# Q, k and v of token blocks two to four as pairs of 64-row matmuls with two PSUM sums each

## The chip, the core and the metric

One core of a Trainium2 chip runs the whole program. Its engines work side by side: TensorE (PE; its weight loads are listed as PEld), VectorE (DVE), ScalarE (ACT), GpSimd (POOL) and SyncE (SP), which issues the DMAs here. TensorE writes its sums to PSUM, which has eight banks of 128 x 512 fp32; VectorE and ScalarE read them. The metric is the device time of one execution in microseconds; the lower the better.

## The reference

```python
x = A_x                                  # 1 x 2048 x 576
xn = layernorm(x)
qkv = xn @ wqkv                          # 576 x 1728, 32 heads of 18
p = softmax(q @ k.T * 18 ** -0.5)
s = (p @ v) @ wo
g = silu((gelu(xn @ w_gate) * (xn @ w_up)) @ w_down)   # 4608 hidden
out = x + s * g
```

Everything is fp32. The kernel works in a reduced-mantissa format (fp32r) on parts: an operand is split into a high part and the low part that is left, and a product is the sum of high by high, low by high and high by low.

## The kernel before

The tokens are cut into NB = 4 blocks of TB = 512, written b = 0 to 3 in the code and first to fourth here. A first stage (the pools `pro` and `pps`) makes the layernorm, transposes xn and computes q, k and v; it stores q and k in DRAM (`qk`) as high and low parts, v in DRAM (`vs`), and the transposed xn (`xhs`). A second stage, some 2240 us long, runs the gate and up products interleaved with attention, and a third the output projection. This change is in the first stage, which ends at about 196 us.

For one block the first stage does this:

- `load_x` fetches four row tiles of x, `norm` (line 203) makes their statistics (`bn_stats`, `bn_aggr`), the reciprocal root, and scales them; the last 64 columns are copied behind each tile, so that the rest of the rows is 128 wide.
- `transposes` (line 234) makes 20 PE transposes into five PSUM tiles `pt`; `split_t` (line 185) splits each into a high part by ScalarE (`xt[0]`) and a low part by VectorE (`xt[1]`). The 576 rows are KT = 4 full tiles and 64 left over; the fifth tile, `xt[2]`, holds the high part of those 64 rows in partitions 0 to 63 and the low part in 64 to 127.
- `project` (line 286) computes one 128-row tile of q or k for the 512 tokens of a block; nine of these per block, in the order `ORDER`. `mm_terms` (line 174) issues 14 matmuls of 128 rows: for each of the four full row tiles high by high, low by high, high by low, and two for the fifth tile, whose 128 rows hold high and low at once. ScalarE takes the sum's high part (`t1`), VectorE the low part (`t2`); both have three buffers (`tmp2`, line 182) and are stored to `qk`.
- `values_of` (line 295) computes v of 128 tokens and half the heads, 288 columns; eight per block, 14 matmuls each. ScalarE copies the sum to one of eight buffers `VN`, which is stored to `vs`.
- `store_xt` (line 246) stores the transposed x of the block; for the first block `load_xd` (line 136) loads it back as `xd`, in 64-row pieces, for the gate and up products; `load_gu` (line 122) fetches the first tile of gate and up weights, `split_gu` splits it.

The loop at line 347 goes through the blocks: nine `project`; `norm` of the next block after the fifth of these; `store_xt`; the next block's `transposes`; eight `values_of`. PE's order is that of the program (`manual_schedule`, line 74). On the other engines a scheduler places the instructions, except those that are wrapped in `keep_in_program_order`: they stay in the order in which the program issues them, among themselves. So before, VectorE may do the norm of a later block as soon as its x has landed. A tile pool with `bufs` = n gives a new tile the buffer of an old one, and the first instruction that writes it waits until the old one has been read.

In the second stage `gate_up` (line 403) already runs pairs: two matmuls of 64 rows, one on the upper and one on the lower half of PE's rows, one after the other in program order and with a sum of their own (`pg`, `pu`). So do the attention scores (`pm`, `pe`, lines 698 and 729) and the down products (`py`, line 465).

Of the kernel before, what the change touches and what calls it, by code (L numbers as in the profile page):

```python
# [8 lines left out]
F32 = mybir.dt.float32  # L9
F32R = mybir.dt.float32r  # L10
AF = mybir.ActivationFunctionType
ALU = mybir.AluOpType
# [42 lines left out]
def f(ap):  # L55
    return ap.bitcast(F32)
# [13 lines left out]
def kernel(ctx: ExitStack, tc: tile.TileContext, x, wqkv, wo, w_gate, w_up, w_down, out):  # L70
# [65 lines left out]
    def load_xd(b, key=None):  # L136
# [11 lines left out]
        return xd  # L148


    TERMS = [(0, k, 0) for k in range(KT)] + [(1, k, 0) for k in range(KT)] + [(0, k, 1) for k in range(KT)] \
        + [(0, KT, 2), (1, KT, 2)]

    FIRST_TERMS = sorted(TERMS[:2 * KT], key=lambda t: 2 * t[1] + 3 * t[0]) + TERMS[2 * KT:]


    with tc.tile_pool(name="pro", bufs=1) as pro, tc.tile_pool(name="pps", bufs=1, space=PSUM) as pps:
# [16 lines left out]
        def mm_terms(o, w, cols, xt, toks, swap=False, terms=TERMS):  # L174

            for i, (wp, k, xp) in enumerate(terms):
                xx = xt[xp][:, k, toks] if xp < 2 else xt[2][:, toks]
                ww = w[wp][:, k, cols] if k < KT else w[2 + wp]
                st, m = (xx, ww) if swap else (ww, xx)
                nc.tensor.matmul(o, st, m, start=(i == 0), stop=(i == len(terms) - 1))  # L180

        def tmp2(name):
            return pro.tile([P, TB], F32R, name=name, tag=name, bufs=3)

        def split_t(pt, k, xt):

            if k < KT:
                nc.scalar.activation(xt[0][:, k, :], pt, AF.Copy)
                nc.vector.tensor_tensor(xt[1][:, k, :], pt, f(xt[0])[:, k, :], op=ALU.subtract)
            else:  # L190
                nc.scalar.activation(xt[2], pt, AF.Copy)
                nc.vector.tensor_tensor(xt[2][HR:P, :], pt[HR:P], f(xt[2])[HR:P, :], op=ALU.subtract)

        def load_x(b):
            keep = tc.keep_in_program_order if b == 1 else lambda i: i
# [4 lines left out]
                xr.append(xx)  # L200
            return xr

        def norm(xr, b, between=None, behind=None):
            keep = tc.keep_in_program_order if b == 1 else lambda i: i
            st = pro.tile([P, 4, 8], F32, name="st", bufs=2)
            for j in range(4):
                bs = pro.tile([P, 2, 6], F32, name="bs", bufs=2)
                for h in range(2):
                    one = nc.vector.bn_stats(bs[:, h, :], xr[j][:, 288 * h:288 * h + 288])  # L209
                    keep(one)  # L210
                if behind and j == 0:
                    behind(one)
                nc.vector.bn_aggr(st[:, j, 0:2], bs)
            var, r, t = st[:, :, 1], st[:, :, 3], st[:, :, 4]
            nc.scalar.activation(t, var, AF.Sqrt, bias=eps)
            if between:
                between()
            nc.vector.reciprocal(r, t)
            nc.vector.scalar_tensor_tensor(t, r, -0.5, r, op0=ALU.mult, op1=ALU.mult)
            nc.vector.scalar_tensor_tensor(t, var, EPS, t, op0=ALU.add, op1=ALU.mult)  # L220
            nc.vector.scalar_tensor_tensor(r, t, 1.5, r, op0=ALU.add, op1=ALU.mult)
            for j in range(4):
                last = nc.vector.tensor_scalar(xr[j][:, 0:D], xr[j][:, 0:D], st[:, j, 0:1], st[:, j, 3:4],
                                               op0=ALU.subtract, op1=ALU.mult)
                nc.scalar.activation(xr[j][:, D:D + HR], xr[j][:, R0:D], AF.Copy)
            return last

        def warm(n):

            o = pps.tile([P, TB], F32, name="po", bufs=3)  # L230
            for i in range(n):
                nc.tensor.transpose(o[:, 0:P], ident, ident)

        def transposes(b, xr):
            xt = XT[b % 2]
            pts = [pps.tile([P, TB], F32, name="pt", bufs=KT + 1) for k in range(KT + 1)]
            for j in range(4):
                if b == 0 and j == 0:
                    warm(46)
                for k in range(KT + 1):  # L240
                    nc.tensor.transpose(pts[k][:, j * P:(j + 1) * P], xr[j][:, k * P:(k + 1) * P], ident)  # L241
            for k in range(KT + 1):
                split_t(pts[k], k, xt)
            return xt

        def store_xt(b, xt):
            keep = tc.keep_in_program_order if b == 0 else lambda i: i
            for i in range(2):
# [1 line left out]
                keep(nc.sync.dma_start(xhs[b][i, R0:D, :], f(xt[2])[HR * i:HR * i + HR, :]))  # L250

        XT = [(pro.tile([P, KT, TB], F32R, name=f"xth{i}"), pro.tile([P, KT, TB], F32R, name=f"xtl{i}"),
               pro.tile([P, TB], F32R, name=f"xtr{i}")) for i in range(2)]
        VN = [pro.tile([P, H // 2, DH + 1], F32, name=f"vn{i}") for i in range(8)]
        eps = pro.tile([P, 1], F32, name="eps")
        nc.vector.memset(eps, EPS)
        for v in VN:
# [26 lines left out]
            WV[c] = hi, lo, VR[0][:, cc], VR[1][:, cc]  # L284

        def project(b, t, xt):
            o = pps.tile([P, TB], F32, name="po", bufs=3)
            mm_terms(o, WQK[t], slice(0, P), xt, all_t, terms=FIRST_TERMS if b == 0 and t == ORDER[0] else TERMS)
            hi, lo = tmp2("t1"), tmp2("t2")
            nc.scalar.activation(hi, o, AF.Copy)  # L290
            nc.vector.tensor_tensor(lo, o, f(hi), op=ALU.subtract)
            for i, a in enumerate((hi, lo)):
                nc.sync.dma_start(qk[i, t * P:(t + 1) * P, b * TB:(b + 1) * TB], f(a))

        def values_of(b, j, c, xt):
            t = b * 4 + j
            o = pps.tile([P, TB], F32, name="po", bufs=3)
            mm_terms(o[:, 0:D // 2], WV[c], slice(0, D // 2), xt, slice(j * P, (j + 1) * P), True)
            v = VN[2 * j + c]
            nc.scalar.activation(v[:, :, 1:DH + 1], o[:, 0:D // 2].rearrange("p (h d) -> p h d", d=DH), AF.Copy)  # L300
            nc.sync.dma_start(vs[t * P:(t + 1) * P, c * H // 2:(c + 1) * H // 2, :], v)

        def split_wo(k):
            n = min(P, D - k * P)
# [31 lines left out]
        last = norm(xr, 0, first_hi, first_loads)  # L336
# [520 lines left out]
    with tc.tile_pool(name="epi", bufs=1, reuse_waits="tile") as epi:  # L857
# [184 lines left out]
```

## Time and profile before

| quantity | value |
|---|---|
| time, median of 3 runs | 2547.44 us (2546.95 to 2547.98) |
| span of the profiled execution | 2545.4 us |
| PE busy in the span | 2538.4 us |
| first stage, start of the first gate and up pair | 196.27 us |
| matmuls of q and k in the trace | 36 products of 14 |
| matmuls of v in the trace | 32 products of 14 |

The span runs from the first to the last instruction of one profiled execution; the time of a run holds what lies around it as well. A line of the profile names the source line (L180), the engine, the operation, the tile written and the tiles read, the shapes and the count; behind the bars stand busy time, the mean duration in ns, and the idle time of the engine just before with what ended it. In the chain of waits each piece has its start, its length and the instructions that set the end. The matmuls of PE overlap, so the distance from one start to the next is its pace, not the duration of one.

### The profile page before, as it was taken

To read this page: it belongs to the slowest core of one execution; us is meant where nothing else is said; L and a number is where in the kernel's file an instruction comes from. 1 tells how busy PE (TensorE), PEld (TensorE's weight loads), DVE (VectorE), ACT (ScalarE), POOL (GpSimd) and SP (SyncE) were. 2 spreads that over 40 slices of the span, in tenths; PEclk is the share of its full clock that TensorE was granted. 3 is DMA by queue.
4 is the path that set the end of the run, shared out by engine and by line. 5 is a ranking of instruction groups with operands and counts; after the bars stand their busy time and mean duration, and the time that the engine had idled before them with its cause. 6 is when DMAs were issued, how large, how long until landed. Compare 5 with 4: busy or idle time off the path is not lost.

```text
span 2545.4 us, 63167 instructions
## 1 busy us (share of the span) xinstructions
PE 2538.4 (100%) x23974; PEld 2008.4 (79%) x23974; DVE 1950.4 (77%) x3499; ACT 1555.1 (61%) x3050; POOL 1320.7 (52%) x1447
## 2 busy tenths in 40 slices
PE   9999999999999999999999999999999999999999
PEld 8888877777777777777777787777777777787798
DVE  5316988888888888888888888888888888887277
ACT  3223366666677666676666677666676666676612
POOL 2117545555465554445565545554446555455675
PEclk9999999999999999999999999999999999999999
DMA  8876444444465444444455444444446444444483
GB/s 267 269 241 158 100 103 106 100 111 109 107 150 121 104 109 112 113 112 110 111 125 140 116 111 106 105 108 112 109 109 153 115 109 109 108 106 99 114 242 107
DMA packets 398686, 325.51 MB, mean 128 GB/s; under 512 B 117408, under 2 KB 309184, under 8 KB 398384
## 3 DMA queue, kind: packets, MB, share of 16 engines
q1 hardware_dynamic: 398384, 321.47, 49.7%
q8 instruction: 191, 3.13, 0.5%
q14 instruction: 111, 0.91, 0.1%
HBM read 266.63 MB, written 54.70 MB: 126 GB/s over the span
## 4 chain that ended last, share of the span: by engine, by line
PE 98%; ACT 1%; DVE 0%; DMA 0%; SPq 0%; issue 0%; ACTq 0%
PE pg L413 29%; PE py L465 18%; PE acc L764 18%; PE pm L698 9%; PE pe L729 9%; PE po L180 7%; PE pu L413 6%; PE po L902 2%; ACT pT L730 1%; PE pt L241 0%; SPq L665 0%; DMA xx<-in_A_x_dram 0%; DVE bs L209 0%; ACT t L426 0%; DMA KS<-qk 0%
## 5 line engine op out<-in xcount | busy, mean ns | idle before, releaser
L730 ACT ACTIVATE pT<-pe 128x512 f32<-128x512 f32 x2048 | 1153.3, 598 | 368.7 <-PE pm L698 226.3
L699 DVE TENSOR_REDUCE mx<-pm 128x1 f32<-128x512 f32 x2048 | 1249.6, 680 | 151.3 <-PE pm L698 149.0
L413 PE MATMUL pg<-xd,wh 64*128 64x512 f32 x2592 | 928.9, 390 | 0.0
L413 PE MATMUL pu<-xd,wh 64*128 64x512 f32 x2592 | 928.6, 390 | 0.0
L698 PE MATMUL pm<-KS,q 64*128 64x512 f32 x2048 | 779.0, 388 | 0.8 <-DMA KS<-qk 0.5
L729 PE MATMUL pe<-q,KS 64*128 64x512 f32 x2048 | 775.2, 387 | 0.0
L413 PEld LDWEIGHTS pg<-xd,wh 64*128 64x128 f32 x2592 | 476.5, 184 | 115.9 <-POOL wh L106 21.1
L413 PE MATMUL pg<-xd,wl 64*128 64x512 f32 x1296 | 501.6, 387 | 0.0
L413 PE MATMUL pu<-xd,wl 64*128 64x512 f32 x1296 | 501.4, 387 | 0.0
L413 PEld LDWEIGHTS pu<-xd,wh 64*128 64x128 f32 x2592 | 477.0, 184 | 2.0
L764 PE MATMUL acc<-pT,VS 128*32 128x512 f32 x4096 | 452.8, 594 | 0.0
L108 POOL TENSOR_TENSOR wl<-raw,wh 128x384 fp32r<-128x384 f32 x432 | 434.2, 1019 | 13.7
L106 POOL TENSOR_SCALAR hh<-t 128x512 fp32r<-128x512 f32 x128 | 79.1, 618 | 652.0 <-DVE t L440 637.8
L698 PEld LDWEIGHTS pm<-KS,q 64*128 64x128 f32 x2048 | 374.2, 184 | 31.1 <-DVE mx L699 4.3
L729 PEld LDWEIGHTS pe<-q,KS 64*128 64x128 f32 x2048 | 370.9, 184 | 21.9
L465 PE MATMUL py<-dh,hh 64*128 64x288 f32 (+1 forms) x2160 | 360.3, 294 | 0.3
L465 PE MATMUL py<-dl,hh 64*128 64x288 f32 (+1 forms) x2160 | 358.7, 292 | 0.0
L465 PE MATMUL py<-dh,hl 64*128 64x288 f32 (+1 forms) x2160 | 358.3, 292 | 0.0
L764 PEld LDWEIGHTS acc<-pT,VS 128*32 128x32 f32 x4096 | 127.4, 110 | 289.9 <-issue 278.0
L106 POOL TENSOR_SCALAR wh<-raw 128x384 fp32r<-128x384 f32 x432 | 217.2, 515 | 143.7 <-PE pu L413 83.4
L453 DVE TENSOR_TENSOR Y<-py,Y 128x288 f32<-128x288 f32 x544 | 227.1, 452 | 59.8 <-PE py L465 52.7
L413 PEld LDWEIGHTS pg<-xd,wl 64*128 64x128 f32 x1296 | 238.7, 184 | 32.1
(119 smaller groups left out, 3106.7 us busy)
## 6 DMA issues: line engine op xcount, KB each, us to landing
KS<-qk SPq DMA_DIRECT2D x1536, 36.0 KB
raw<-in_B_w_gate_dram SPq DMA_DIRECT2D x144, 288.0 KB
raw<-in_B_w_up_dram SPq DMA_DIRECT2D x144, 288.0 KB
raw<-in_B_w_down_dram SPq DMA_DIRECT2D x67, 576.0 KB
VS<-vs SPq DMA_DIRECT2D x128, 152.0 KB
qk<-t SPq DMA_DIRECT2D x72, 256.0 KB
q<-qk SPq DMA_DIRECT2D x384, 36.0 KB
xx<-in_A_x_dram SPq DMA_DIRECT2D x32, 288.0 KB
```

The source lines that it names most:

```text
L106: first = nc.gpsimd.tensor_scalar(hi, raw, 1.0, 1.0, op0=ALU.mult, op1=ALU.mult)
L108: low_part[:] = [keep(nc.gpsimd.tensor_tensor(lo, raw, f(hi), op=ALU.subtract))]
L180: nc.tensor.matmul(o, st, m, start=(i == 0), stop=(i == len(terms) - 1))
L413: nc.tensor.matmul(o, w[1 + wp][k][rr, c, :], xd[xp][k][rr, c, :], start=(i == 0), stop=(i == len(terms) - 1))
L453: one = kept(nc.vector.tensor_tensor(yy, py, yy, op=ALU.add))
L465: return nc.tensor.matmul(py, hs[g][a][rr, j * P:(j + 1) * P], wd[w][rr, g, 288 * c:288 * c + 288], start=start, stop=stop)
L698: nc.tensor.matmul(pm, QS[u, r][rr, t * P:(t + 1) * P], KS[(u * NA + c) % KB][r][rr, :], start=True, stop=True)
L699: nc.vector.tensor_reduce(MX[u][:, 2 * r + a, t, c:c + 1], pm, axis=AX.X, op=ALU.max)
L729: nc.tensor.matmul(pe, KS[(u * NA + c) % KB][r][rr, t * P:(t + 1) * P], QS[u, r][rr, :], start=True, stop=True)
L730: nc.scalar.activation(PT[u, kt][:, 2 * r + a, :], pe, AF.Exp, scale=SCALE)
L764: nc.tensor.matmul(ACC[u][32 * a:32 * a + 32, :], VS[(u * NA + c) % VB][:, v:v + 32], pt[:, a, :], start=first, stop=last, skip_group_chec ...
L902: nc.tensor.matmul(po, parts_of(b, j)[x_][:, k, :], OW[w][c][k], start=(i == 0), stop=(i == len(OUT) - 1))
```

## The change

In blocks two to four each product of q, k and v is made of matmuls of 64 rows. `product` gives it two PSUM sums, one for the rows 0 to 63 of every tile and one for 64 to 127, and appends the matmuls to two lists, `HALVES`; as long as both lists hold something, one matmul of each is issued in turn. For the 64 left-over rows `split_t` now makes two tiles, `xt[2]` with high above low and `xt[3]` with low above high; `REST` names the three 64-row products (high by high, low by high, high by low) that are spread over the two halves as 2 + 1 or 1 + 2, in turn. So a product has 27 matmuls, 14 in one half and 13 in the other, and every second product leaves one matmul that pairs with the first of the next product. `put`, called when the last matmul of a product has been issued, evicts: for q and k ScalarE copies the first sum, VectorE adds the second, ScalarE takes the high part, VectorE the low part; for v a copy and an add. All of these are kept in program order on ScalarE and VectorE. The norm is cut into `norm_stats` and `norm_rest`, for blocks two and three at the places given below and kept in program order. PSUM has one set of eight tiles `po` for sums and transposes. The first block's products stay whole (`whole_product`); they too draw on the set of eight. `VN` has five buffers for eight, and `load_xd` stands one block later in the program.

```diff
-    TERMS = [...] + [(0, KT, 2), (1, KT, 2)]
+    TERMS = [(0, k, 0) for k in range(KT)] + [(1, k, 0) for k in range(KT)] + [(0, k, 1) for k in range(KT)]
+    REST = [[[(0, KT, 2), (1, KT, 2)], [(0, KT, 2)]], [[(0, KT, 3)], [(0, KT, 3), (1, KT, 3)]]]
...
+        def product(shape, operands, put, terms=TERMS):
+            pos = [pps.tile([P, TB], F32, name="po", bufs=8)[:, 0:shape] for _ in range(2)]
+            parity = PRODUCTS[0] % 2
+            PRODUCTS[0] += 1
+            left = [0]
+            for a in range(2):
+                mine = terms + REST[parity][a]
+                left[0] += len(mine)
+                for i, term in enumerate(mine):
+                    def step(a=a, i=i, term=term, n=len(mine)):
+                        st, m = operands(slice(HR * a, HR * a + HR), *term)
+                        nc.tensor.matmul(pos[a], st, m, start=(i == 0), stop=(i == n - 1))
+                        left[0] -= 1
+                        if left[0] == 0:
+                            put(*pos)
+                    HALVES[a].append(step)
+            while all(HALVES):
+                for half in HALVES:
+                    half.pop(0)()
...
+        def ordered(b, i):
+            if b:
+                tc.keep_in_program_order(i)
+            return i
...
-                nc.scalar.activation(xt[2], pt, AF.Copy)
-                nc.vector.tensor_tensor(xt[2][HR:P, :], pt[HR:P], f(xt[2])[HR:P, :], op=ALU.subtract)
+                for i, (hi, lo) in enumerate((HALF, HALF[::-1])[:2 if b else 1]):
+                    ordered(b, nc.scalar.activation(xt[2 + i], pt, AF.Copy))
+                    ordered(b, nc.vector.tensor_tensor(xt[2 + i][lo, :], pt[lo], f(xt[2 + i])[lo, :], op=ALU.subtract))
...
-        VN = [pro.tile([P, H // 2, DH + 1], F32, name=f"vn{i}") for i in range(8)]
+        VN = [pro.tile([P, H // 2, DH + 1], F32, name=f"vn{i}") for i in range(5)]
...
+            def put(o, o2):
+                hi, lo = tmp2("t1"), tmp2("t2")
+                both = f(lo) if b else o
+                if b:
+                    ordered(b, nc.scalar.activation(both, o, AF.Copy))
+                    ordered(b, nc.vector.tensor_tensor(both, both, o2, op=ALU.add))
+                ordered(b, nc.scalar.activation(hi, both, AF.Copy))
+                ordered(b, nc.vector.tensor_tensor(lo, both, f(hi), op=ALU.subtract))
+                for i, a in enumerate((hi, lo)):
+                    nc.sync.dma_start(qk[i, t * P:(t + 1) * P, b * TB:(b + 1) * TB], f(a))
...
+            def put(o, o2):
+                vv = v[:, :, 1:DH + 1]
+                ordered(b, nc.scalar.activation(vv, o.rearrange("p (h d) -> p h d", d=DH), AF.Copy))
+                if b:
+                    ordered(b, nc.vector.tensor_tensor(vv, vv, o2.rearrange("p (h d) -> p h d", d=DH), op=ALU.add))
+                nc.sync.dma_start(vs[t * P:(t + 1) * P, c * H // 2:(c + 1) * H // 2, :], v)
...
-                if n == 4 and b + 1 < NB:
-                    norm(xr, b + 1)
+                if b + 1 < NB and n == (4 if b == 0 else 5):
+                    st = pro.tile([P, 4, 8], F32, name="st", bufs=2)
+                    norm_stats(xr, b + 1, st, range(4) if b == 0 else range(2))
+                    if b == 0:
+                        norm_rest(xr, 1, st)
+                if 0 < b < NB - 1 and n == 6:
+                    norm_stats(xr, b + 1, st, range(2, 4))
+                if 0 < b < NB - 1 and n == 7:
+                    norm_rest(xr, b + 1, st)
...
-            if b == 1:
+            if b == 2:
                 XD = load_xd(0)
...
+        last_steps()
```

More of the change, by code (lines that the diff above doesn't have):

```diff
@@ L172, in load_rows @@
             return raw
[L174 to L180, printed above, removed]
+        HALVES = [[], []]
+        PRODUCTS = [0]
+        def product(shape, operands, put, terms=TERMS):
[17 more added lines that the diff above has]
+                    half.pop(0)()
@@ new lines, in last_steps, with whole_product @@
+        def last_steps():
+            for half in HALVES:
+                while half:
+                    half.pop(0)()
+        WHOLE = [(0, KT, 2), (1, KT, 2)]
+        def whole_product(shape, operands, put, terms=TERMS):
+            o = pps.tile([P, TB], F32, name="po", bufs=8)[:, 0:shape]
+            mine = terms + WHOLE
+            for i, term in enumerate(mine):
+                st, m = operands(slice(0, P), *term)
+                nc.tensor.matmul(o, st, m, start=(i == 0), stop=(i == len(mine) - 1))
+            put(o, None)
@@ L201, in load_x, with norm_stats @@
             return xr
[L203 to L206, printed above, removed]
+        def norm_stats(xr, b, st, js, behind=None):
+            keep = tc.keep_in_program_order if b else lambda i: i
+            for j in js:
                 bs = pro.tile([P, 2, 6], F32, name="bs", bufs=2)
@@ L212, in norm, with norm_rest, keep @@
                     behind(one)
-                nc.vector.bn_aggr(st[:, j, 0:2], bs)
+                ordered(b > 1, nc.vector.bn_aggr(st[:, j, 0:2], bs))
+        def norm_rest(xr, b, st, between=None):
+            def keep(i):
+                return ordered(b > 1, i)
             var, r, t = st[:, :, 1], st[:, :, 3], st[:, :, 4]
-            nc.scalar.activation(t, var, AF.Sqrt, bias=eps)
+            keep(nc.scalar.activation(t, var, AF.Sqrt, bias=eps))
             if between:
                 between()
[L218 to L221, printed above, removed]
+            keep(nc.vector.reciprocal(r, t))
+            keep(nc.vector.scalar_tensor_tensor(t, r, -0.5, r, op0=ALU.mult, op1=ALU.mult))
+            keep(nc.vector.scalar_tensor_tensor(t, var, EPS, t, op0=ALU.add, op1=ALU.mult))
+            keep(nc.vector.scalar_tensor_tensor(r, t, 1.5, r, op0=ALU.add, op1=ALU.mult))
             for j in range(4):
-                last = nc.vector.tensor_scalar(xr[j][:, 0:D], xr[j][:, 0:D], st[:, j, 0:1], st[:, j, 3:4],
-                                               op0=ALU.subtract, op1=ALU.mult)
-                nc.scalar.activation(xr[j][:, D:D + HR], xr[j][:, R0:D], AF.Copy)
+                last = keep(nc.vector.tensor_scalar(xr[j][:, 0:D], xr[j][:, 0:D], st[:, j, 0:1], st[:, j, 3:4],
+                                                    op0=ALU.subtract, op1=ALU.mult))
+                keep(nc.scalar.activation(xr[j][:, D:D + HR], xr[j][:, R0:D], AF.Copy))
             return last
         def warm(n):
-            o = pps.tile([P, TB], F32, name="po", bufs=3)
+            o = pps.tile([P, TB], F32, name="po", bufs=8)
             for i in range(n):
@@ L235, in transposes @@
             xt = XT[b % 2]
-            pts = [pps.tile([P, TB], F32, name="pt", bufs=KT + 1) for k in range(KT + 1)]
+            pts = [pps.tile([P, TB], F32, name="po", bufs=8) for k in range(KT + 1)]
             for j in range(4):
@@ L242, in transposes @@
             for k in range(KT + 1):
-                split_t(pts[k], k, xt)
+                split_t(pts[k], k, xt, b)
             return xt
@@ L252 @@
         XT = [(pro.tile([P, KT, TB], F32R, name=f"xth{i}"), pro.tile([P, KT, TB], F32R, name=f"xtl{i}"),
-               pro.tile([P, TB], F32R, name=f"xtr{i}")) for i in range(2)]
-        VN = [pro.tile([P, H // 2, DH + 1], F32, name=f"vn{i}") for i in range(8)]
+               pro.tile([P, TB], F32R, name=f"xtr{i}"), pro.tile([P, TB], F32R, name=f"xtq{i}")) for i in range(2)]
+        VN = [pro.tile([P, H // 2, DH + 1], F32, name=f"vn{i}") for i in range(5)]
         eps = pro.tile([P, 1], F32, name="eps")
@@ L286, in project, with operands @@
         def project(b, t, xt):
[L287 to L293, printed above, removed]
+            def operands(rr, wp, k, xp):
+                return w_part(WQK[t], rr, k, wp, slice(0, P)), x_part(xt, rr, k, xp, all_t)
@@ L295, in values_of @@
+            if b:
+                product(TB, operands, put)
+            else:
+                whole_product(TB, operands, put, FIRST_TERMS if t == ORDER[0] else TERMS)
         def values_of(b, j, c, xt):
             t = b * 4 + j
[L297 to L300, printed above, removed]
@@ L303, in split_wo @@
+            (product if b else whole_product)(D // 2, operands, put)
         def split_wo(k):
@@ L335 @@
         xr = load_x(0)
-        last = norm(xr, 0, first_hi, first_loads)
+        st = pro.tile([P, 4, 8], F32, name="st", bufs=2)
+        norm_stats(xr, 0, st, range(4), first_loads)
+        last = norm_rest(xr, 0, st, first_hi)
         raw, (raw_r, rest) = ahead_qk.pop(0)[1], ahead_qk.pop(1)
```

19 lines of the change are left out of this document (13 added, 6 removed).

## The prediction

> **What bounds the kernel now.** First the page's busy times and its chain of waits, then the same chain cut to the first 200 us, where the changed lines run.
>
> ```profile
> span 2545.4 us, 63167 instructions
> PE 2538.4 (100%) x23974; PEld 2008.4 (79%) x23974; DVE 1950.4 (77%) x3499; ACT 1555.1 (61%) x3050; POOL 1320.7 (52%) x1447
> PE 98%; ACT 1%; DVE 0%; DMA 0%; SPq 0%; issue 0%; ACTq 0%
> ```
>
> ```profile
> 41.85 2.18 PE pt L241 x20
> 44.04 44.32 PE po L180 x238
> 88.36 2.18 PE pt L241 x20
> 90.54 44.31 PE po L180 x238
> 134.85 2.18 PE pt L241 x20
> 137.04 59.23 PE po L180 x350
> 196.27 0.43 PE pg L413
> ```
>
> TensorE (PE) never waits from the end of the first block (41.85) to the first gate and up section (196.27). A piece of 44.3 us is the values of one block (8 products of 14 matmuls, 288 columns) and q and k of the next (9 of 14, 512 columns). All later work is on PE too, so what PE gains or loses here moves the end by as much.
>
> Two PE timelines give the interval from one matmul to the next: whole ones in the second block, then pairs of 64-row ones from the middle of the kernel.
>
> ```profile
> 57.48 0.69 PE L180 MATMUL po<-vl,xth 128*128 128x288 f32 x4
> 58.01 0.69 PE L180 MATMUL po<-vh,xtl 128*128 128x288 f32 x4
> ...
> 58.80 1.09 PE L180 MATMUL po<-xth,qh 128*128 128x512 f32 x4
> 59.73 1.10 PE L180 MATMUL po<-xth,ql 128*128 128x512 f32 x4
> 60.66 1.10 PE L180 MATMUL po<-xtl,qh 128*128 128x512 f32 x4
> ```
>
> ```profile
> 1000.31 0.39 PE L729 MATMUL pe<-q,KS 64*128 64x512 f32 x1
> ...
> 1008.24 0.39 PE L413 MATMUL pg<-xd,wh 64*128 64x512 f32 x1
> 1008.47 0.29 PE L465 MATMUL py<-dh,hh 64*128 64x288 f32 x2
> ...
> 1010.84 0.29 PE L465 MATMUL py<-dh,hh 64*128 64x288 f32 x2
> ```
>
> Whole: 0.93 us for 4, 0.2333 us each; 288 columns 0.53 for 4, 0.1333. Pairs: 35 between 1000.31 and 1008.24, 0.2266; 288 columns 18 in 2.37, 0.1317. So a pair costs slightly less than one whole matmul.
>
> **PE's work.** In blocks two to four a product goes from 14 whole matmuls to 27 half ones, 13.5 pairs (the low-by-low product goes, and the last odd half pairs with the next product's first). Per block, 512 columns: 126 x 0.2333 = 29.40 becomes 121.5 x 0.2266 = 27.53; 288 columns: 112 x 0.1333 = 14.93 becomes 108 x 0.1317 = 14.22. That is -2.6 a block, **-7.7** in all. If in these lines a pair takes as long as a whole matmul, -4.8.
>
> Changing between whole and half matmuls has a price, seen at a change from whole down products to pairs:
>
> ```profile
> 220.15 0.29 PE L465 MATMUL py<-dh,hl 128*128 128x288 f32 x1
> 220.37 0.49 PE L413 MATMUL pg<-xd,wh 64*128 64x512 f32 x1
> ...
> 220.71 0.39 PE L413 MATMUL pg<-xd,wl 64*128 64x512 f32 x1
> ```
>
> 0.22 and 0.34 us stand where 0.13 and 0.23 would: 0.2 a change. The edit adds five (into the second block's pairs, in and out around two sets of transposes) and saves the one before the sections: **+0.8**.
>
> **Evictions and the norm.** Two sums need, for q and k, ScalarE copy, VectorE add, ScalarE high part, VectorE low part. The nearest rows are the evictions of before, and the norm of the fourth block's x on VectorE:
>
> ```profile
> L291 DVE TENSOR_TENSOR t<-po,t 128x512 fp32r<-128x512 f32 x36 | 24.9, 691 | 86.0 <-ACT t L290 76.7 <-DMA qk<-t 6.7 <-DMA raw<-in_A_wo_dram 2.6
> L290 ACT ACTIVATE t<-po 128x512 fp32r<-128x512 f32 x36 | 21.4, 596 | 77.8 <-PE po L180 65.3 <-DMA qk<-t 9.6 <-issue 2.5
> L300 ACT ACTIVATE vn<-po 128x288 f32<-128x288 f32 x32 | 13.2, 418 | 40.0 <-PE po L180 40.0
> ```
>
> ```profile
> 99.84 0.82 DVE L209 BATCH_NORM_STATS2 bs<-xx 128x6 f32<-128x288 f32 x2 [5.86 <-DMA xx<-in_A_x_dram]
> 100.69 0.21 DVE L213 BATCH_NORM_AGGREGATE st<-bs 128x2 f32<-128x12 f32 x1
> ...
> 106.13 0.18 DVE L218 RECIPROCAL st<-st 128x4 f32<-128x4 f32 x1 [0.51 <-ACT st L215]
> ...
> 106.96 2.05 DVE L223 TENSOR_SCALAR xx<-xx,st 128x576 f32<-128x576 f32 x4
> ```
>
> The four steps take 0.60 + 0.69 + 0.60 + 0.69 = 2.6 us, under a product's 13.5 x 0.2266 = 3.06, and eight PSUM banks let PE run ahead: hidden as such. Values take a copy and an add, 0.42 and at most 0.69 of 13.5 x 0.1317 = 1.78 us: hidden too. Not so the norm. Before, it runs at 99.84 to 109, 26 us ahead of its transposes (134.85). In the changed program VectorE's order in the second block is: product 5's steps, all four statistics (1.06 each, 4.2), product 6's, product 7's, then the rest of the norm (0.8 from the reciprocal to the scaling, about 0.6 for the first tile). VectorE, ScalarE and the transposes queue behind every wait in this list.
>
> If only PE held it up: the pairs start at 58.80 + 0.2, product 5 ends at 77.4; + 2.6 + 4.2 + 2.0 + 2.0 (VectorE's add to its low part, twice) + 0.8 + 0.6 = 89.6. The transposes are due at 58.80 + 0.2 + 27.53 = 86.5: 3.0 late at the least.
>
> **The store queue** adds to it. The first copy of product p overwrites a buffer (three of each) that the store of p-3 must have left. The queue during the values of the first block, q and k of the second, and in the first block:
>
> ```profile
> 44.04:58.80 14.76, 14.76 (x112) 14.76 (x112) 5.20 (x8) 6.30 (x15) 0.00 (x0) 1.00 0.94 318
> 58.80:88.36 29.56, 29.56 (x130) 23.77 (x129) 12.38 (x28) 6.19 (x14) 4.39 (x3) 1.00 0.90 302
> 20.00:42.00 22.00, 22.00 (x97) 17.71 (x96) 10.82 (x28) 5.36 (x12) 8.45 (x9) 1.00 0.93 266
> ```
>
> ```profile
> qk<-t SPq DMA_DIRECT2D x19, 256.0 KB
> xhs<-xth SPq DMA_DIRECT2D x2, 1024.0 KB
> xhs<-xtl SPq DMA_DIRECT2D x2, 1024.0 KB
> xd<-xhs SPq DMA_DIRECT2D x4, 384.0 KB
> vs<-vn SPq DMA_DIRECT2D x8, 152.0 KB
> xx<-in_A_x_dram SPq DMA_DIRECT2D x4, 288.0 KB
> xhs<-xtr SPq DMA_DIRECT2D x4, 128.0 KB
> ```
>
> The last two columns: it is 90 to 94% busy at 302 to 318 GB/s. SyncE's order in the changed program puts all six loads of `xd` between the stores of products 0 to 3 (now they reach to the block's end), and the first gate and up tile (2 x 288 KB) into the first block. From 44.04 to the landing of product 3's stores it moves 5 `qk` stores left over (1280 KB), two blocks' `xhs` (4608), 8 of `vs` (1216), 4 of x (1152), 8 of `qk` (2048), 6 of `xd` (2304): 12608 KB, 12.9 MB, 40.6 to 42.7 us at these rates, so 84.6 to 86.8; with gate and up (0.59 MB, 1.9 us) about 87.6. Product 2's stores, 1280 KB earlier, land at 83.4. Product 5's copy waits for these: 83.4 + 2.6 + 4.2 + 2.0 + 2.0 + 0.8 + 0.6 = 95.6, which is 9.1 late; without gate and up in the way 7.2. I take **+8**; the bounds are 3.0 (queue not felt) and 16 (266 GB/s: 13.5 MB by 94.8, 7.2 later). The same 1.9 us meet the last split of the value weights in the first block, which I put at about 1 us to spare: **+1.0** (0 to 2).
>
> **Three smaller waits.** Behind each set of transposes the first value product needs banks that ScalarE and VectorE must first empty, 0.60 + 0.69 less the odd half matmul and the change of mode: 0.8, twice, **+1.6**. At the second set the rest of the norm stands before product 7's steps: it starts after product 6's steps and two statistics (2.6 + 2.1), is 0.5 late, and the fifth transposed tile needs the bank that ScalarE empties only behind the four tail copies, some 1.6 later: **+2.1** (0 to 4). Five value buffers for eight wait on stores of 152 KB, 0.5 us each at the rate above: nothing, at most 1.
>
> **Sum**: -7.7 + 0.8 + 8 + 1.0 + 1.6 + 2.1 = +5.8. The span goes from 2545.4 to 2551.2; the median of the runs stands 2.0 above this span: **2553.2 us**.
>
> **Rivals.**
> 1. *The queue is not felt.* PE runs four products ahead and the loads might fall into gaps. For it: in the trace of before the copies wait 9.6 us for stores, all told; against: 0.90 busy before anything is added. The second block's stall is 3.0, the first block's 0: -0.2, 2547.2.
> 2. *The clock.* PE would stand still some 8 us. The kernel's start shows a cold array:
>
> ```profile
> 1.35 7.25 PE L232 MATMUL po<-ident 128*128 128x128 f32 x46 [1.35 <-POOL ident masks.py:199]
> ```
>
> 46 transposes in 7.25, against 2.18 for 20 later (0.109 each, 5.0 for 46): 2.2 us lost. If the pause cools it again, the transposes behind it pay this: +8.0, 2555.4. Against: no pause of before is long enough to show it. [...]
> 3. *The gain shows.* If VectorE is through in time (the statistics slip into its gaps, the stores land early), stalls shrink to about 1.5: -7.7 + 0.8 + 1.5, 2542.0. For it: VectorE is idle half of each product; against: its order is fixed.
> 4. *A pair is no shorter than a whole matmul*: 2.9 more than the sum, 2556.1. Against: two rows above, both of pairs.
>
> **How the numbers follow.** Likeliest 0.45 (its own range +2.5 to +9, 2550 to 2556.5), rival 1 0.20, rival 2 0.17, rival 3 0.13, rival 4 0.05. 0.2%, about what a measurement of this kernel can tell from no change, is 5.1 us. Faster: 0.10 of rival 3. Slower: 0.30 of the likeliest, with rivals 2 and 4, 0.52. The same: 0.15 of the likeliest, rival 1, and 0.03 of rival 3: 0.38. The range for 8 in 10 leaves out the best of rival 3 and ends where 266 GB/s alone would bring it (+8): 2543.5 to 2561.
>
> **What would show it.** Right: PE idle once, for 6 to 10 us, ahead of the third block's transposes, released by VectorE's scaling; ScalarE's first copies in the second block waiting for `qk` stores; 0.2266 and 0.1317 per pair. Wrong: no such gap (rival 1 or 3), transposes at 0.21 us each behind it (rival 2), pairs at 0.233 (rival 4), or a wait in the sections behind 196 that this sum does not have.

## The result, and the profile after

| | before | after |
|---|---|---|
| median of 5 runs | 2547.67 us | 2558.9 us |
| profiled span | 2545.4 us | 2557.6 us |

The ratio is 1.0045, with a 95% interval of 1.0033 to 1.0057: slower by 11.2 us. The page's busy times of the kernel after, and shares of its chain of waits:

```profile
span 2557.6 us, 64610 instructions
PE 2538.0 (99%) x24637; PEld 2006.8 (78%) x24637; DVE 1988.5 (78%) x3550; ACT 1573.4 (62%) x3080; POOL 1324.4 (52%) x1447
PE 94%; DMA 2%; DVE 1%; ACT 1%; SPq 1%; issue 1%; POOL 0%; ACTq 0%; POOLq 0%
```

PE's busy time is the same to 0.4 us (2538.4 before), though half matmuls were taken out. The span is 12.2 us longer, and the chain now leaves PE for 6% of it. The chain cut to the first 232 us, start and length of each piece, shows where:

```profile
42.81 1.11 PE po L293 x10
43.91 0.57 ACT t L349
44.49 0.58 ACT vh L116
45.11 0.76 DVE vl L117
45.91 14.72 PE po L213 x108
60.63 12.86 PE po L191 x108
73.49 0.60 ACT t L347
74.11 0.33 DVE t L348
74.44 8.82 DMA qk<-t
83.34 0.61 ACT t L347
...
95.74 0.59 DVE xx L275
96.47 3.66 PE po L293 x16
...
193.16 4.36 DMA qk<-t
197.60 0.61 ACT t L347
198.24 0.70 DVE t L348
198.98 2.01 PE po L191 x26
201.27 6.16 DMA vs<-vn
...
208.42 0.47 DVE vn L370
```

Before, this was PE alone from 41.85 to 196.27. Now it runs over the split of the value weights in the first block, then over a `qk` store (8.82 us) to product 5's copy at 83.34 (products of a block are counted from 0 to 8) and through the norm to the scaling at 95.74, and once more over stores near the end. The chain lists product 3's copy and add ahead of that store; but of three buffers product 5's copy takes the one of product 2, so the store that it waits for is product 2's. The PE timeline has the waits in brackets, with what ended them:

```profile
96.47 4.39 PE L293 MATMUL po<-ident,xx 128*128 128x128 f32 x20 [7.33 <-DVE xx L275]
...
144.78 0.63 PE L293 MATMUL po<-ident,xx 128*128 128x128 f32 x4 [0.15 <-DVE xx L275]
146.93 1.97 PE L293 MATMUL po<-ident,xx 128*128 128x128 f32 x16 [1.52 <-ACT t L347]
...
151.63 0.67 PE L191 MATMUL po<-vh,xth 64*128 64x288 f32 x6 [0.67 <-DVE xtl L236]
...
208.05 0.47 PE L495 MATMUL pg<-xd,wh 64*128 64x512 f32 x1
209.02 0.46 PE L495 MATMUL pu<-xd,wh 64*128 64x512 f32 x1 [0.51 <-DVE vn L370]
```

The starts in the same view of before:

```profile
41.69 2.34 PE L241 MATMUL pt<-ident,xx 128*128 128x128 f32 x20
...
88.19 2.35 PE L241 MATMUL pt<-ident,xx 128*128 128x128 f32 x20
...
196.20 0.50 PE L413 MATMUL pg<-xd,wh 64*128 64x512 f32 x1
```

Set against these (and 134.69 for the fourth block's transposes), PE is 0.96 us late at the second block's transposes (42.65), 8.28 at the third's, 10.09 at the fourth's and 11.85 at the first gate and up section; the span ends 12.2 later. Nearly all is lost in the first 210 us.

The third block's 20 transposes took 4.39 us where they had taken 2.35. The busy times by stretch (the third-last column is the granted clock) show why:

```profile
89.13:93.79 4.66, 0.01 (x2) 0.00 (x0) 3.73 (x10) 1.25 (x3) 0.00 (x0) 1.00 0.16 62
93.79:100.61 6.82, 4.14 (x20) 4.12 (x20) 3.33 (x9) 2.17 (x7) 0.00 (x0) 0.50 0.53 181
```

After 4.7 us without a matmul the granted clock fell to 0.50 for 6.82 us. And a pair's pace, from the third block's q and k:

```profile
119.07 1.18 PE L191 MATMUL po<-xth,qh 64*128 64x512 f32 x8
120.01 1.18 PE L191 MATMUL po<-xth,ql 64*128 64x512 f32 x8
120.94 1.19 PE L191 MATMUL po<-xtl,qh 64*128 64x512 f32 x8
```

Eight half matmuls, four pairs, start every 0.935 us: 0.2338 us a pair, against 0.2333 for a whole matmul before. So the only saving is that a product takes 13.5 of them instead of 14, which is 4.6 us over three blocks. Last, ScalarE's longest waits from 60.5 to 210 (total, times, longest):

```profile
ACT t L347 <- PE po L191: 25.4, 18, 3.0
ACT t L349 <- DVE t L348: 23.9, 27, 3.3
ACT t L347 <- DMA qk<-t: 15.3, 5, 5.7
```

The copies waited 15.3 us for `qk` stores: three times in the second block (8.3 us) and twice in the last.

### The profile page after: what moved, and what is told of

It is laid out like the page before. It is cut to its first block, busy times and chain, and to the rows that moved or that the text cites. A ratio compares the mean times of both kernels' runs of the same rounds, so it can differ in the third digit from the quotient of the medians.

```text
span 2557.6 us, 64610 instructions
## 1 busy us (share of the span) xinstructions
PE 2538.0 (99%) x24637; PEld 2006.8 (78%) x24637; DVE 1988.5 (78%) x3550; ACT 1573.4 (62%) x3080; POOL 1324.4 (52%) x1447
## 4 chain that ended last, share of the span: by engine, by line
PE 94%; DMA 2%; DVE 1%; ACT 1%; SPq 1%; issue 1%; POOL 0%; ACTq 0%; POOLq 0%
PE pg L495 29%; PE py L547 18%; PE acc L846 18%; PE pm L780 9%; PE pe L811 9%; PE pu L495 5%; PE po L191 3%; PE po L984 2%; PE po L213 2%; ACT pT L812 1%; DMA qk<-t 1%; DMA vs<-vn 0%; PE po L293 0%; DVE bs L256 0%; SPq L747 0%
```

## The experiments

The theory: the third block's transposes wait because product 5's copy is late (the store queue) and because the norm stands in VectorE's order behind it; the pause cools the clock on top. Each run was timed five rounds against the kernel before on the same chip. Ratios are to the kernel before. The runs were made in three groups on three chips, on which the kernel before took 2547.2 to 2548.0 us; so times of different groups are compared to about 1 us only.

### Which part of the wait is the queue

**Both loads late.** The `xd` loads and the first gate and up tile are put behind the third block's stores:

```diff
-                XD = load_xd(0)
+                XD = load_xd(0, last_store[0])
-                ahead = load_gu(0, tc.keep_in_program_order)
+                ahead = load_gu(0, lambda i: tc.keep_in_program_order(late(i)))
```

(`late` lets a load be issued only behind `last_store`, the last `xhs` store of the third block.)

> The six loads of xd and the first gate and up tile are issued behind the third block's store of its transposed x; nothing else moves. Theory A (the third block's transposes come late because the copies wait for the store queue): product 5's copy comes when PE is through with it, at about 60.8 + 6 x 3.16 = 79.7 instead of 83.34, and the steps behind it (2.6, four statistics 3.7, twice 2.0, 1.4 to the first scaled tile) end at 91.4, where PE is ready at 89.1: the wait falls from 7.33 to about 2.5 us, so the clock does not cool (2.2 less) and the first block loses its 0.9 us stall. Time 2558.9 - 4.8 - 2.2 - 0.9, about 2551. Theory B (the two-sum evictions and VectorE's order alone make the wait, the queue only fills idle time): the wait stays above 6 us and the time at 2558.

2555.5 us (1.0032, 1.0020 to 1.0045; single runs 2553.39 to 2559.42). Its PE timeline at the two sets of transposes, and the clock behind each:

```profile
91.02 3.95 PE L293 MATMUL po<-ident,xx 128*128 128x128 f32 x20 [2.52 <-DVE xx L275]
...
139.78 0.63 PE L293 MATMUL po<-ident,xx 128*128 128x128 f32 x4 [0.72 <-DVE xx L275]
141.93 3.61 PE L293 MATMUL po<-ident,xx 128*128 128x128 f32 x16 [1.52 <-ACT t L353]
```

```profile
90.90:94.30 3.40, 3.28 (x16) 3.31 (x17) 1.44 (x3) 1.03 (x4) 0.00 (x0) 0.51 0.31 86
...
142.10:145.40 3.30, 3.30 (x16) 3.04 (x15) 1.91 (x4) 1.90 (x4) 0.00 (x0) 0.50 0.37 145
```

The wait fell to 2.52 us, as theory A said, and no copy of the second block waits for a store any more. So of 7.33 us the queue made 4.8 and the order alone 2.5. What was wrong is the clock: it cooled at 2.5 us too, and this time at the fourth block's transposes as well, which took 3.2 of the 4.5 us by which the time missed the expected 2551 (3.95 and 3.61 us, where 2.35 and 1.97 are usual).

**The gate and up tile late, alone**, with the second half of that edit:

> Only the first gate and up tile (576 KB) is issued late, behind the third block's stores; the six loads of xd stay between the stores of products 0 to 3. Theory A (the prediction's terms): the first block's stall of 0.9 us goes and the queue ahead of product 5's copy is 1.9 us shorter, so the third block's transposes start 1.9 us earlier in all, at about 94.5; the pause is still over 5 us, so they stay slow. Time 2558.9 - 1.9, about 2557. Rival (this tile is the whole of the queue's part): the time of the run with both loads late, 2555.5.

2557.8 us (1.0041, 1.0029 to 1.0054). The transposes start at 95.36 with a wait of 6.79 us and take 4.50; PE leaves the first block without the stall. The time is 1.1 us lower, less than these runs resolve; in the traces the third block's transposes start 1.11 us earlier and the first gate and up section 0.74. So the term was there, at about half its size.

**The loads of `xd` late, alone**, with the first half:

> Only the six loads of xd (2304 KB, 7.4 us at 318 GB/s) are issued late; the first gate and up tile stays in the first block. Theory A: that is more than the queue's part of the wait (7.33 - 2.52 = 4.8 us in the run with both late), so the wait falls to about 2.5 us as there, and the first block's stall of 0.9 us stays: 2556.4. Rival (the gate and up tile matters more): above 2557.5.

2553.8 us (1.0027, 1.0016 to 1.0037), below the expected 2556.4. The wait is 2.52 us, as with both loads late: the six loads of `xd` make nearly all of the queue's part. The first block's stall is still there (waits of 0.41 and 0.54 us). The time is not higher than with both loads late, though; in the profiled executions transposes ran slow at one set here (3.25 us for the 20; the last 16 of the fourth block's took 1.97), not at two.

### The norm's place

**Norm early.** Statistics behind products 1 and 2, the rest behind product 3:

```diff
-                if b + 1 < NB and n == (4 if b == 0 else 5):
+                if b + 1 < NB and n == (4 if b == 0 else 1):
...
-                if 0 < b < NB - 1 and n == 6:
+                if 0 < b < NB - 1 and n == 2:
...
-                if 0 < b < NB - 1 and n == 7:
+                if 0 < b < NB - 1 and n == 3:
```

> The norm of the third and fourth block's x stands behind products 1, 2 and 3 instead of 5, 6 and 7; the queue is as in the changed kernel. Theory A: the copies of products 4 to 6 still wait some 8 us for stores, but the transposes now need only a bank, product 7's first copy at about 91: the wait falls from 7.33 to 2 or 3 us, the clock stays warm (2.2 less), and the second set loses its 1.5 us wait. Time 2558.9 - 4.8 - 2.2 - 1.5, about 2550.4. If the queue alone set the wait (rival), the wait would stay above 6 us and the time above 2557; if the norm's place alone set it, the wait would vanish and the time be 2546 to 2548.

2549.95 us (1.0008, 0.9999 to 1.0016), as theory A had it. The wait for the scaling is gone; one for a bank is left, 0.82 us where 2 or 3 were expected:

```profile
90.04 0.90 PE L293 MATMUL po<-ident,xx 128*128 128x128 f32 x4
91.77 1.97 PE L293 MATMUL po<-ident,xx 128*128 128x128 f32 x16 [0.82 <-ACT t L347]
```

**Norm early and both loads late**, the two edits together:

> Both: norm behind products 1 to 3, loads of xd and of the first gate and up tile behind the third block's stores. Theory A: no wait ahead of the third block's transposes, none of 1.5 us ahead of the fourth block's, no stall of 0.9 in the first block, a warm clock: 2558.9 - 7.3 - 2.2 - 1.5 - 0.9, about 2547.0, the time of the kernel before within 1 us, so the pairs' saved matmul time (4.7 us for three blocks at 0.2333 and 0.1333 a pair) is still spent on changes of mode and on waits for banks behind the transposes. If the evictions of two sums are themselves too slow for PE, a wait of 3 us or more stays and the time is above 2550.

2548.4 us (1.0004, 0.9996 to 1.0013), 10.5 us below the changed kernel and level with the one before. From the first block's end to the first gate and up section no PE wait longer than 0.7 us is left. Order and queue together are the loss, with the clock that they cooled.

### The clock

**Transposes in the pause.** 60 transposes of the identity, into a bank that the first real one overwrites:

```diff
+                if b == 2 and j == 0:
+                    for i in range(60):
+                        nc.tensor.transpose(pts[0][:, 0:P], ident, ident)
```

> 60 more transposes of the identity, into the bank that the first real transpose overwrites, run on PE while it waits ahead of the third block's transposes (60 x 0.109 = 6.5 of 7.3 us). If the pause cooled the clock, the 20 transposes take about 2.2 to 2.4 us instead of 4.39 (four scaled tiles arrive 0.5 us apart, so not much below 2.2), some of it lost again to the wait for the first low parts: 2557.0 to 2557.5, and the granted clock of that stage goes from 0.72 to 1.00. If they are slow for another reason (the tiles arrive one by one, the tail copies), they keep 4.4 us and the time stays at 2558.9.

2559.7 us (1.0048, 1.0034 to 1.0062): not faster, though the stage did what theory A said. Its PE timeline there, and ScalarE's in the last block:

```profile
96.47 2.40 PE L296 MATMUL po<-ident,xx 128*128 128x128 f32 x20 [0.97 <-DVE xx L275]
...
149.96 0.80 PE L191 MATMUL po<-vh,xth 64*128 64x288 f32 x7 [0.67 <-DVE xtl L236]
...
208.00 0.38 PE L498 MATMUL pg<-xd,wh 64*128 64x512 f32 x1
```

```profile
197.57 0.60 ACT L350 ACTIVATE t<-po 128x512 f32<-128x512 f32 x1 [6.67 <-DMA qk<-t]
```

The transposes are back at 2.40 us, at a granted clock of 1.00 from 96.40 to 99.90, and PE is at the fourth block's values at 149.96 instead of 151.63. Yet the first gate and up section starts at 208.00, as before the edit (208.05): product 8's copy in the last block starts at 197.57 against 197.60, because the store it waits for lands no earlier. The cold clock was real and cost 2 us where it stood; the last block's queue would have taken these 2 us anyway.

**Both loads late, and transposes in the pauses** (20 ahead of the third block's set, 6 and 12 at the fourth's):

> As the run with both loads late, with transposes of the identity in the pauses: 20 ahead of the third block's transposes, 6 ahead of the fourth's and 12 between its fourth and fifth. Theory A (there the short pauses of 2.52 and 0.72 + 1.52 us halved the clock for 3.41 us each, and a dip that comes in some executions and not in others makes its wide spread, 2553.4 to 2559.4): the third block's 20 transposes take 2.4 us instead of 3.95, the last 16 of the fourth's 2.0 instead of 3.6, the granted clock stays 1.00, about 2552.5, and the executions lie within 2 us of each other. Rival (the saved time is waited for elsewhere, as in the run with 60 transposes): 2555.

2553.7 us (1.0024, 1.0015 to 1.0034), single runs 2552.21 to 2555.52. The two sets took 2.40 and, for the last 16, 1.97 us; the clock stayed at 1.00. The spread fell from 6.0 to 3.3 us, not to the 2 expected. Of 3.2 us saved at the transposes the medians show 1.8, with intervals that overlap, and the first gate and up section starts 0.93 us earlier (202.42 against 203.35): in the last block a copy (0.7 us) and an add (0.3 us) now hold PE up, as in the run with 60 transposes. So theory A was right at the transposes, and part of the gain went the rival's way.

### The pairs themselves

**Whole products, the rest as in the changed kernel**:

```diff
-            if b:
-                product(TB, operands, put)
-            else:
+            if 1:
                 whole_product(TB, operands, put, FIRST_TERMS if b == 0 and t == ORDER[0] else TERMS)
...
-            (product if b else whole_product)(D // 2, operands, put)
+            whole_product(D // 2, operands, put)
```

(The second sum's copy and add and the second fifth tile `xt[3]` go with it.)

> The changed kernel with whole products in all blocks (one sum, one copy and one subtraction per product); the norm behind products 5, 6 and 7 and the early loads as in the changed kernel. Theory A (the wait is made of the late copy of product 5 plus the steps in VectorE's order behind it): the steps behind that copy shrink from 13.1 us (83.34 to 96.47) to 1.3 + 3.7 + 1.3 + 1.3 + 0.8 + 0.6 = 9.0 and PE comes 1 us later, so the wait falls from 7.3 to about 2.2 us and the second set's goes; matmul time rises by 4.7 us: 2558.9 - 5.1 - 1.5 - 2.2 + 4.7, about 2555, or 2557 if a 2 us pause still cools the clock. Theory B (the queue's backlog alone sets the end of the wait): the transposes start at 96 as before and the time is 2562.

2549.9 us (1.0008, 0.9999 to 1.0017), far below both. No wait is left ahead of either set of transposes, and ScalarE's copies wait for PE alone:

```profile
ACT t L349 <- PE po L213: 21.6, 8, 2.8
ACT xx L277 <- DVE xx L275: 2.6, 4, 1.9
```

The expectation failed because the edit moved more than it named: with other lengths of work SyncE's order changed too. Only three `xd` loads stand before product 7's stores, where the changed kernel has all six before product 3's. So this run undoes queue and evictions together. Beside the run with both loads late (no store waits either, pairs, 2.52 us of wait and a cooled clock) it shows what makes the order's part: mostly the longer chain of two-sum steps. With one copy and one subtraction the norm is through in time where it stands; PE also comes 0.7 us later there (89.20 against 88.50), so this chain makes some 1.8 of the 2.52 us.

**Whole products with norm early and both loads late**:

> As the run with the norm early and the loads late, but blocks two to four use whole products again (one sum, one copy and one subtraction, the low-by-low product of the last 64 rows computed as in the kernel before); the second fifth tile is left out. Theory A: pairs at 0.2333 and 0.1333 us save 4.7 us of matmul time and give back 0.8 for changes of mode and about 2.5 in waits for banks, so whole products are about 1 us slower here: 2549.4. Rival (a pair takes longer than a whole matmul, or the two-sum evictions cost PE more than that): 2547 or less.

2547.85 us (1.0000, 0.9991 to 1.0009), beside 2548.4 with pairs: no difference that these runs resolve. In the traces the stretch from the second block's transposes to the first gate and up section is 153.94 us with pairs (42.48 to 196.42) and 154.79 with whole products (42.20 to 196.99), so the pairs keep 0.85 of 4.6 us there. Where most of the rest stays can be read in the run with pairs: each set of transposes is followed by a value product that waits for a bank (0.55 and 0.70 us), and a pair in the third block waits 0.21 us for an add. From start to start these three places cost 0.9, 1.05 and 0.5 us more than the pace, and around the transposes stand changes of mode.

### Trying to keep the gain

**Transposes behind product 6**, with norm early and both loads late:

```diff
+                if 0 < b < NB - 1 and n == 6:
+                    nxt = transposes(b + 1, xr)
...
-            nxt = transposes(b + 1, xr) if b + 1 < NB else None
+            if b == 0:
+                nxt = transposes(1, xr)
```

> As the run with the norm early and the loads late, and in the second and third block the next block's transposes run behind product 6 instead of product 8, so that products 7 and 8 (6.3 us) cover the emptying of their banks. Theory A (what is left of the loss after that run is the wait of the first value product for the transposes' banks, steps of 1.04 and 1.00 us where 0.13 is due): both go, 2548.4 - 1.8, about 2546.6, below the kernel before. Rival (that time turns up again somewhere else, the queue of the last block above all): 2548.4 as before.

2548.7 us (1.0007, 0.9998 to 1.0016): the rival. A bank is still waited for after the third block's set (0.55 us), and the fourth block's transposes now wait 0.51 us for an add and 0.82 us for a copy.

**The same with the queue as it was**:

> Norm early and transposes behind product 6 as in the first kernel of this group, but the loads of xd and of the first gate and up tile stand where the changed kernel has them. Theory A (the queue costs by itself, whatever stands behind it): the first block's stall of 0.9 is back and the copies of products 4 to 6 again wait 8 us in all for stores; PE's lead of three products in eight banks takes most of it, so about 2 us more than the first kernel of this group: 2548.5. Rival (with the norm out of the way the queue is not felt at all): 2546.6.

2553.1 us (1.0020, 1.0011 to 1.0028). The queue costs 4.4 us here, twice what theory A said and all that its rival denied: waits of 1.22, 0.39, 0.82 and 1.72 us stand one behind the other from 83.65 to 91.30, and the clock cools:

```profile
89.00:92.20 3.20, 1.48 (x12) 0.95 (x12) 3.20 (x4) 2.30 (x5) 1.10 (x1) 1.00 0.52 186
92.20:95.60 3.40, 3.40 (x20) 2.66 (x18) 2.71 (x5) 1.08 (x2) 0.00 (x0) 0.50 0.93 216
```

**No odd half behind the transposes** (norm early, both loads late):

```diff
+            last_steps()
             nxt = transposes(b + 1, xr) if b + 1 < NB else None
```

> As the run with the norm early and both loads late, but the odd half matmul of product 8 runs alone ahead of the transposes instead of paired behind them, so that product 8's two banks are emptied during the transposes and the first value product does not need the first transposed tile's bank. Theory A: the steps of 1.04 and 1.00 us behind the two sets of transposes become 0.13, three unpaired halves cost 0.1 to 0.2 each: 2548.4 - 1.8 + 0.4, about 2547.0. Rival (as with the transposes moved early, the time is waited for elsewhere): 2548.5.

2548.5 us (1.0004, 0.9995 to 1.0013): the rival again. The bank wait behind the third block's set is gone, the fourth's stayed (0.70 us), and the first gate and up section starts at 195.85, 0.57 us earlier. Further on PE then waits for the first down products (1.91 us, against 0.11 with norm early and both loads late alone):

```profile
218.56 0.40 PE L554 MATMUL py<-dl,hh 128*128 128x288 f32 x1 [1.91 <-POOL dl L113]
```

The chain behind this wait is a load of `w_down` (6.15 us, landing at 214.6) that SyncE issues behind the attention's loads, its split on ScalarE, and GpSimd. In this execution the 0.57 us are lost there. Whether any gain of the first stage would be is not shown: the chain goes back to PE's own work at 202.22, and with both loads late, where the stage ends 7 us later, the down products wait too (1.50 us at 225.94). No version measured here beats the kernel before.

## Why the prediction was right, and where its sum was off

The direction and the likeliest mechanism held: 2553.2 was forecast and 2558.9 came, inside the range, 11.2 us above the kernel before where 5.5 was said. But it lies outside the likeliest case's own range (2550 to 2556.5). Rivals 2 and 4 were priced as if each stood in place of the likeliest case, and both came together with it; two of the signs named for being wrong showed, transposes at 0.21 us each behind the gap and pairs at 0.234. That the time still fell into the range is owed to the bound on the queue that set its upper end, not to these terms.

A wait in brackets is PE's idle time. From start to start such a place costs more: matmuls of a stream overlap by some 0.16 to 0.25 us (before, four took 1.09 us and the next four started 0.93 after them; in the pairs at 119.07 it is 1.18 and 0.94), and the interval behind a wait or a change of mode is 0.1 us longer than the pace (0.23 us at 101.52 and at 198.98, where 0.13 is due). By the prediction's steps:

- **The wait ahead of the third block's transposes, +8.** Measured 7.33 idle, 7.5 from start to start, released by VectorE's scaling, with the split that the prediction gave: 3.0 by order alone (2.52 with both loads late) and the rest by the store queue (4.8). Product 5's copy came at 83.34, to 0.1 us the time worked out from the queue's bytes. Part of the agreement is luck: PE was through 2.6 us later than said (89.1 for 86.5), and the transposes could start 0.9 later (96.5 for 95.6).
- **The first block's stall, +1.0.** Measured 0.7: the value weights' split ends at 45.87, and PE, 0.96 us late as the values start (44.75, 43.79 before), is 1.66 late at their last two matmuls (60.20, 58.54 before). With the gate and up tile late it goes.
- **PE's work, -7.7.** This is the mis-sized term. A pair took 0.2338 us, not 0.2266, and 0.1333 at 288 columns, not 0.1317: 3 x (121.5 x 0.0072 + 108 x 0.0016) = 3.1 us less gain, -4.6. That is rival 4, at 0.05, though its price was 2.9. The rows it was argued away with are pairs of another part of the kernel; the nearer row was the whole matmul in the very lines that change.
- **Changes of mode, +0.8.** The one that stands apart from any wait, into the second block's pairs, cost 0.2 as said (0.22 and 0.33 us where 0.13 and 0.23 are due). The others stand beside waits and are counted with these.
- **The clock** (rival 2, 0.17, +2.2): it came, at 2.0 us (4.39 for the 20 transposes with the clock at 0.50 up to 100.61, 2.40 at 1.00 with 60 more ahead of them). It was set up as an alternative to the likeliest case though its only premise, a pause of some 8 us, was that case's own forecast. Its chance was the author's estimate, and what was said against it overlooked the end of the trace of before: there, behind PE's last matmul, the clock was 1.00 from 2541.60 to 2545.00 and 0.50 from 2545.02 to 2545.43, the end of the span. In the changed kernel 7.33 us of idling did the same with work still to come.
- **Banks behind the transposes, +1.6, and the second set, +2.1.** Idle 0.24 and 0.67 us for the first, 0.15 + 1.52 for the second, the 1.52 released by ScalarE's copy as said: 2.6 in all. From start to start, with the changes of mode there, it is 0.7 at the third block's set and 3.2 at the fourth's.
- **Five value buffers, nothing to 1.** In the last block copies into them wait for their stores (one piece of the chain is 6.16 us of `vs`); the last value's add comes at 208.42, and the first up matmul waits 0.51 us for it, 0.6 from start to start beyond what that place took before.
- **The store queue in the last block** has no term in the sum. Product 8's copy waits there for a `qk` store and its add holds PE up for 0.33 us at 198.98, 0.9 from start to start. The same queue stood ready to take back any gain, as the run with 60 transposes shows.

With the terms as measured from start to start: -4.6 + 0.2 + 7.5 + 0.7 + 2.0 + 0.7 + 3.2 + 0.6 + 0.9 = +11.2. The 0.96 us that PE is late already at the second block's transposes make it 12.2, which is the difference of the spans, to the few tenths that such a count is good for. Of the 0.96, 0.85 stand at the first transposes of all (9.03 to 9.88), outside the prediction's sum; in the twelve runs they start between 9.3 and 10.0. In the changed kernel 0.45 of it is a wait of VectorE for a tile of x, and the rest is open.

## What to carry to other kernels

Ask of every rival whether it replaces the forecast or follows from it: what follows from it belongs into the sum. Price an operation from the lines that change, and when a step gets longer on an engine with a fixed order, add up what stands behind it in that order and in the store queue; here these two, at 2.5 and 4.8 us, outweighed all the matmul time saved. And a saving on the bounding engine has to get past the next waits: here 4.6 us less matmul time came to nothing measurable even without the long wait, most of it spent on banks and changes of mode.

## What the hardware showed beside this

The granted clock fell to half behind some of PE's waits and not behind others. In the changed kernel it was 0.50 from 93.79 to 100.61, with 7.33 us of waiting ahead of the transposes. With both loads late it was 0.51 from 90.90 to 94.30, at a wait of 2.52 us, and 0.50 from 142.10 to 145.40, behind 0.72 and 1.52 us with four transposes between them. With the transposes early and the queue as it was it stayed at 1.00 through waits of 1.22, 0.39 and 0.82 us and was 0.50 from 92.20 to 95.60, behind one of 1.72 us. It stayed at 1.00 behind 0.15 and 1.52 us in the changed kernel (144.00 to 152.00). With no odd half behind the transposes the down products behind a wait of 1.91 us ran at 0.13 us each (218.93 to 219.99), as they do at full clock, and the mean clock of that execution was 1.000. So the length of one wait does not tell these cases apart: 1.72 us was enough in one and 1.91 us was not in another. What does is not shown.

One and the same wait of 2.52 us gave 3.95 us for the 20 transposes with both loads late and 3.25 with the loads of `xd` late alone. The slow stretch lay differently against them: in the first the 64x512 matmul behind the transposes took 0.49 us as usual (94.90), in the second 0.79 (95.60). In three digits the mean clock sets only the slowest of the executions with both loads late apart: 0.998 at 2559.42 us, 0.999 at the other four (2553.39 to 2556.84).

Pairs of 64-row matmuls did not run at one pace: 0.2338 us in q and k, 0.2266 at 1000 us in the gate and up products and the scores, both with 512 columns. How far apart the two halves of a pair start does not go with it: under 0.01 us in the second block's q and k and 0.09 in the third's, both at 0.234; under 0.01 us at 1000 us in the kernel before and 0.03 there in the changed one, both at 0.2266. What sets the pace was not tried.
